# A planned attention and feed-forward kernel on one core: another build-time order for the first pairs, 26 early transfers begun by ScalarE, and one small VectorE instruction replaced

## The chip, the cores and the metric

The kernel runs on one NeuronCore of one Trainium2 chip. The metric is the device time of one execution in microseconds. Before the change it was 673.36, 673.85 and 676.03 us in three runs; the median is 673.85.

## What is computed

```python
batch, n_heads, seq, head_dim = (4, 8, 768, 48)
...
for t in range(S):
    kt, vt, bt = (k_n[:, :, t], v[:, :, t], beta[:, :, t, None])
    y[:, :, t] = np.einsum('bhd,bhde->bhe', q[:, :, t], state)
    v_old = np.einsum('bhde,bhd->bhe', state, kt)
    state = state + bt[:, :, :, None] * np.einsum('bhd,bhe->bhde', kt, vt - v_old)
...
h = x @ w_in
g = h * np.cos(h)
return (g @ w_out).astype(np.float32)
```

First comes a delta-rule attention: k_n is k divided by its norm plus 1e-6, and a state of 48 x 48 per batch and head is corrected at every one of the 768 steps. Its output, laid out as 3072 tokens of 384 numbers, is x of a feed-forward block with 2048 hidden columns and the gate h cos h. The feed-forward weights arrive as 64-bit floats, read as pairs of 32-bit words.

## The kernel before

**Units and pairs.** The sequence is cut into 24 units of 32 steps, and two units make a pair. Within a unit the recurrence is solved as a triangular system. For one pair the products of its keys (`gram`, L591) are scaled on VectorE (`gram_keys`, L602), written to DRAM (`gram_put`, L629) and fetched back in another layout (`gram_get`, L638); there a column-by-column elimination makes the inverse (`invert`, L667 and L674, 31 columns of two instructions each). It runs on VectorE for pair 0, and on GpSimd for all others. The result is written to DRAM (`put`, L683; for pair 0 ScalarE first copies it, L678) and fetched back for each unit (`get`, L692, four transfers). Then, on TensorE: `state` (old state times keys and queries, L709), `solve` (L740), `update` (L763), `within` (L780) and `features` (a transpose, L799). VectorE stands between them with the right side (L724), `u` (L750) and the new state (L771). So each unit waits for the one before it.

**Norms.** ScalarE squares k (L495), VectorE sums (L500), GpSimd takes the root (L512), and VectorE makes the scales; its first instruction there adds 1e-6 to the norm (L523, a tensor_scalar).

**Feed-forward.** A weight block comes in as word pairs (`narrow_load`, L460), is split on ScalarE (L468, L470), shifted on VectorE (L474, L479), and added on GpSimd (L483). There are 28 blocks: 0 to 11 are w_in, 12 to 27 are w_out. For pairs 0 and 1 the hidden layer is computed plainly (`hidden`, L820, eight blocks for each pair); block k of a unit needs the w_in adds up to 3k + 2. ScalarE and VectorE make the gate from it (`turns`, `rest`, `cos`, `gate`, L860 to L876). The output of pair 0 is plain too (`output`, L962): its first block of columns needs w_out adds 12 to 15. All later products use seven multiplications instead of eight, with sums made by VectorE (L936, L955, L1019, L1035).

**What sets the order.** Class `Order` is a planner that runs while the program is built. Every step is added with an engine, a cost, a due time and its dependencies. `run` plays the steps through, each time taking for a free engine the ready step that is due first, and emits the instructions in that order; at the end every instruction is tied to the one before it on its engine (`pin`). So each engine works through a fixed order, and the planner's costs and due times reach the chip only through it. `NUDGE` moves due times by kind of step, `STICK` lets TensorE stay with small-tile or with large steps a little longer, and transfers are modelled with eight in flight. All early transfers are issued by SyncE, except the first two q loads (eight transfers) on ScalarE and the constants on GpSimd. In the built program each transfer waits for the transfer that stands eight places before it, whichever queue began it. Tiles with tag `g` (eight buffers) are shared by the word pairs, the squares and the gates.

```python
    IN_FLIGHT, ISSUE = 8, 0.49
...
            for engine, heap in ready.items():
                if free[engine] > now:
                    continue
                able = [x for x in heap if x[0] <= limit and fits(x[2])]
                item = min(able, default=None)
```

Of the kernel before, what the change touches and what calls it, by code (L numbers as in the profile page):

```python
# [46 lines left out]
class Order:  # L47
# [9 lines left out]
    WINDOW = 818.445  # L57
    LAG = {"PE": 0.2, "DVE": 0.15, "ACT": 0.15, "POOL": 0.2, "SP": 2.0, "IN": 0.0}
    IN_FLIGHT, ISSUE = 8, 0.49
# [3 lines left out]
    STICK = 1.823  # L63
    CHANGE = 0.15

    EARLY, NUDGE = 6, {('state', True): -3.4, ('features', False): -48.4, ('left', True): 37.6, ('solve', True): -19.7, ('turn', False): 12.2, ('within', True): -6.1, ('features_out', True): 39.0, ('rest', False): -12.6, ('weigh', False): -49.2, ('gram_put', True): 12.6, ('collect', False): -26.2, ('within', False): -32.5, ('features', True): -14.4, ('gate', True): -24.7, ('layer_out', False): -12.4, ('update', True): -10.5, ('sum', False): 24.3, ('layer', False): -1.8, ('add', True): -24.4, ('cos', True): 15.7, ('update', False): -6.1, ('solve', False): -34.1, ('norms', True): -9.2, ('state', False): -9.6, ('sum', True): 20.5, ('right', True): 24.7, ('hidden', True): 17.1, ('blocks', False): 2.6, ('gram', False): -8.1, ('inv_out', False): -15.0, ('v', False): 17.4, ('out', True): -13.0, ('eye', True): -0.5, ('features_out', False): -17.0, ('within_out', False): -0.6, ('gram_get', False): 12.2, ('gram_get', True): -21.0, ('turns', True): 8.1, ('scale', True): 5.8, ('k', True): -20.2, ('shift', True): -4.8, ('shift', False): 2.4, ('collect', True): 0.5, ('out', False): 0.3, ('scale', False): -1.8, ('out_out', True): 0.9, ('weigh', True): 5.0, ('store', True): -5.1, ('split', False): 9.0, ('within_out', True): -1.7, ('turns', False): -10.9, ('store_right', True): 3.6, ('turn_out', True): 1.5, ('k', False): 0.9, ('store_right', False): -5.1, ('inv', False): 5.4, ('square', False): 7.4, ('square', True): 4.1, ('norms', False): -1.3, ('store', False): 3.3, ('hidden', False): -4.1, ('cos', False): 3.4, ('x_sum', False): -0.6, ('beta_home', False): -1.9, ('store_left', True): -3.3, ('get', False): -6.1, ('get', True): 4.0, ('in_sums', False): 2.9, ('gram_queries', True): 1.6, ('turn_out', False): 5.0, ('update_out', False): -0.3, ('store_left', False): 0.1, ('inv', True): 1.1, ('v', True): -0.9, ('eye', False): -2.2, ('x_sum', True): 0.7, ('split', True): -3.1, ('beta_home', True): -4.7, ('weights', True): -0.3, ('gate', False): -3.7, ('put', False): -1.3, ('inv_out', True): -1.1, ('gram_keys', True): 0.6, ('solve_out', False): -1.5, ('add', False): 1.0, ('in_sums', True): 0.3}
# [19 lines left out]
    def add(  # L86
        self, key, engine, cost, emit, deps=(), makes=(), uses=(), moves=0.0, due=1e9
    ):

        assert key not in self.tasks, key  # L90
        self.tasks[key] = [engine, cost, due, emit, set(deps), makes, uses, moves]
        for t in uses:
            self.users[t] = self.users.get(t, 0) + 1
        for tag, t in makes:
            self.tiles[t] = tag
# [7 lines left out]

    def stall(self, key, now, commit):
# [5 lines left out]
        for i in range(self.written + 1, self.written + n + 1):  # L110
            t = now + cost * (i - self.written) / n + stall
            if (i + self.PHASE + self.AHEAD) % self.BLOCK == 0:
                there[(i + self.PHASE + self.AHEAD) // self.BLOCK + 1] = t + self.FETCH
# [10 lines left out]
    def run(self, wrote):  # L124
# [16 lines left out]
        for key, task in self.tasks.items():  # L141
# [3 lines left out]
            task[2] += self.NUDGE.get((key[0], n < self.EARLY), 0.0)  # L145
# [6 lines left out]
        flights, dma_free, hot = [5.5] * 4 + [8.5] * 4, 8.0, 1e9  # L152
        running, small = {}, False
        events = [(t, 0, None, False) for t in sorted(set(free.values()) | {0.0})]
# [3 lines left out]
        while events:  # L158
# [28 lines left out]
            for engine, heap in ready.items():  # L187
                if free[engine] > now:
                    continue
                able = [x for x in heap if x[0] <= limit and fits(x[2])]  # L190
# [39 lines left out]
                if moves:  # L230
                    end, parts = now, max(1, round(cost / self.ISSUE))
                    for _ in range(parts):
                        end = max(end, flights[-self.IN_FLIGHT]) + self.ISSUE
                        dma_free = max(dma_free, end + 0.5) + moves / parts
                        flights.append(dma_free + 1.4)
                    done = flights[-1]
# [12 lines left out]
def kernel(  # L249
# [70 lines left out]
    def quarter(b):  # L320
        return slice(C * b, C * b + C)
# [31 lines left out]

    def load(n, what="kqv", eng=nc.sync):
# [52 lines left out]
    nc.vector.memset(halves, 0.5)  # L407
    halfpi = const.tile([128, 1], FP, name="halfpi")
# [47 lines left out]
    def narrow_load(t):  # L456
# [3 lines left out]
        nc.sync.dma_start(out=words[t], in_=src)  # L460
# [58 lines left out]
    def scale(m, part):  # L519
# [3 lines left out]
        nc.vector.tensor_scalar_add(knrm, knrm, 1e-6)  # L523
# [94 lines left out]
    def gram_put(n):  # L618
# [9 lines left out]
        for rows, heads, bs in parts:  # L628
            nc.sync.dma_start(  # L629
# [3 lines left out]
    def gram_get(m):  # L633
# [3 lines left out]
        for a in range(SPLIT):  # L637
            nc.sync.dma_start(  # L638
# [42 lines left out]
    def put(m):  # L681
        z_drs[m] = dram.tile([ROWS, SPLIT, 2, H, B, C], FP, name="z_dr")
        nc.sync.dma_start(  # L683
# [3 lines left out]
    def get(n):  # L687
# [3 lines left out]
        for b in range(B):  # L691
            nc.sync.dma_start(out=zts[n][quarter(b)], in_=z_dr[b])  # L692
# [403 lines left out]
    W_IN, W_OUT, LOADS = 24.824, 4.888, 290.255  # L1096
    ONES, PLAIN = range(2), range(1)
    outs_done, collected, layered = [None], [None], [None]
    START = 41.528
    FIRST, STEP = 2.12, 3.854  # L1100
    BASE = [START + (8 * FIRST + (p - 1) * 8 * STEP if p else 0) for p in range(NU // 2 + 2)]

    def inverse(m):
        add(("gram_get", m), "SP", 1.2, lambda: gram_get(m),
            [("gram_put", 2 * m), ("gram_put", 2 * m + 1)], makes=[("gb", ("gb", m))],
            uses=[("g_dr", m)], moves=1.6)
# [372 lines left out]
```

## Time and profile before

| what | value |
|---|---|
| median of three runs | 673.85 us |
| the profiled execution | 673.89 us |
| its span, first to last instruction | 672.1 us |
| TensorE busy | 612.8 us, 91% |
| VectorE, ScalarE, GpSimd busy | 476.5, 295.7, 346.5 us |
| granted TensorE clock, mean | 0.992 |
| moved by DMA | 52.56 MB in 215516 packets, 206948 of them under 512 B |
| instructions | 27308 |

The profiled execution took 1.8 us more than its span. A profile of this kind gives, for each engine, the time in which it executed something, so an engine that is not busy may be waiting or have nothing to do; the waits say for whom. "PEld" is the loading of weights into TensorE, which overlaps its products. A line number is that of the kernel printed above; with SyncE ("SPq") the lines are those of the issued transfers. The table of stretches gives busy microseconds of each engine between two points of the span. A wait named "issue" is one for which the profile shows no releaser.

### The profile page before, as it was taken

What the parts mean: (1) busy time and instruction counts of PE and PEld (TensorE: products, weight loads), DVE (VectorE), ACT (ScalarE), POOL (GpSimd) and SP (SyncE); (2) the same over time, 40 slices, a digit from 0 to 9 for tenths busy, and PEclk for the clock granted to TensorE, in tenths of its full rate; (3) what the DMA queues carried; (4) which work ended last, traced back from release to release, by engine and by line L of the source; (5) the groups of instructions that cost most, each with busy time, mean ns of one, the idle gap of its engine ahead of it and who ended that gap; (6) DMA issues with size and microseconds to landing.
All of it is one profiled execution on the core that took longest, in us unless ns stands there. A gap on an engine that the chain in (4) does not pass through costs nothing.

```text
span 672.1 us, 27308 instructions
## 1 busy us (share of the span) xinstructions
PE 612.8 (91%) x11864; PEld 573.4 (85%) x11864; DVE 476.5 (71%) x911; ACT 295.7 (44%) x510; POOL 346.5 (52%) x734
## 2 busy tenths in 40 slices
PE   4303798999999999999999999999999999999996
PEld 3203786896999998999999999999999999999996
DVE  5799588978676785886876876776666656656661
ACT  4432457672153543653443444444434434434530
POOL 4369878976858328586285482582481670000000
PEclk9999798999999999999999999999999999999999
DMA  8897755455463453534524524515213202000000
GB/s 180 200 207 163 171 116 154 115 98 92 70 101 63 68 87 63 101 44 69 106 39 64 110 33 66 109 25 90 52 22 60 52 6 55 1 5 24 1 24 24
DMA packets 215516, 52.56 MB, mean 78 GB/s; under 512 B 206948, under 2 KB 210164, under 8 KB 215396
## 3 DMA queue, kind: packets, MB, share of 16 engines
q1 hardware_dynamic: 212964, 49.98, 38.7%
q8 instruction: 93, 1.52, 0.9%
q10 hardware_dynamic: 2176, 0.39, 0.4%
q0 software_dynamic: 256, 0.44, 0.3%
q14 instruction: 27, 0.22, 0.1%
HBM read 39.76 MB, written 11.01 MB: 76 GB/s over the span
## 4 chain that ended last, share of the span: by engine, by line
PE 83%; SPq 4%; DMA 4%; POOL 3%; issue 2%; DVE 2%; ACT 1%; ACTq 0%; POOLq 0%
PE p_h L936 29%; PE p_out L1019 28%; PE p_h L820 5%; PE p_kq L709 4%; PE p_out L962 3%; PE p_s L763 3%; PE p_u L740 3%; PE p_kq L780 3%; PE p_g L591 2%; PE p_o L1019 2%; SPq L369 1%; PE p_z L799 1%; SPq L692 1%; POOL knrm L512 1%; DMA zt<-z_dr 1%
## 5 line engine op out<-in xcount | busy, mean ns | idle before, releaser
L667 POOL TENSOR_TENSOR part<-z,gb 128x126 f32<-128x126 f32 (+22 forms) x341 | 132.3, 388 | 108.2 <-DMA gb<-g_dr 47.0
L674 POOL TENSOR_TENSOR z<-z,part 128x126 f32<-128x126 f32 (+22 forms) x341 | 139.9, 410 | 26.7
L936 PE MATMUL p_h<-x_ffn,w_in 128*128 128x128 f32 x1120 | 143.6, 276 | 0.1
L936 PEld LDWEIGHTS p_h<-x_ffn,w_in 128*128 128x128 f32 x1120 | 135.5, 192 | 1.4 <-issue 0.2
L1019 PE MATMUL p_out<-w_out,g_ffn 128*128 128x192 f32 x672 | 123.8, 329 | 0.1
L1019 PEld LDWEIGHTS p_out<-w_out,g_ffn 128*128 128x128 f32 x672 | 107.5, 190 | 1.2
L860 ACT ACTIVATE turns<-p_h 128x512 int32<-128x512 f32 x96 | 56.9, 595 | 101.0 <-DVE p_h L955 74.6
L1019 PE MATMUL p_out<-w_sum,g_ffn 128*128 128x192 f32 x496 | 91.5, 329 | 0.0
L872 ACT ACTIVATE turns<-turns 128x512 f32<-128x512 f32 x96 | 60.4, 629 | 45.1 <-DVE turns L865 44.9
L1019 PEld LDWEIGHTS p_out<-w_sum,g_ffn 128*128 128x128 f32 x496 | 79.3, 190 | 0.9
L876 DVE TENSOR_TENSOR g_ffn<-turns,p_h 128x512 f32<-128x512 f32 x96 | 65.4, 682 | 18.8 <-ACT turns L873 18.0
L865 DVE SCALAR_TENSOR_TENSOR turns<-p_h,turns 128x512 f32<-128x512 f32 x96 | 65.5, 684 | 16.3 <-ACT turns L860 16.0
L1035 DVE TENSOR_TENSOR g_ffn<-g_ffn 128x512 f32<-128x512 f32 x88 | 62.6, 712 | 13.6 <-PE p_out L1019 13.0
L512 POOL TENSOR_TENSOR knrm<-ksum,halves 128x16 f32<-128x16 f32 (+1 forms) x14 | 36.3, 2598 | 66.8 <-DVE ksum L500 66.8
L873 ACT ACTIVATE turns<-turns,halfpi 128x512 f32<-128x512 f32 x96 | 69.3, 722 | 3.1
L955 DVE TENSOR_TENSOR p_h<-g_ffn,p_h 128x512 f32<-128x512 f32 x60 | 41.7, 695 | 38.8 <-PE p_h L936 32.8
L952 ACT COPY g_ffn<-p_h 128x512 f32<-128x512 f32 x60 | 35.0, 583 | 74.8 <-PE p_h L936 74.6
L820 PE MATMUL p_h<-x_ffn,w_in 128*128 128x128 f32 x384 | 48.3, 284 | 0.4 <-issue 0.4
L820 PEld LDWEIGHTS p_h<-x_ffn,w_in 128*128 128x128 f32 x384 | 45.7, 198 | 1.8 <-issue 0.8
L1069 DVE SCALAR_TENSOR_TENSOR o<-p_out,o 128x192 f32<-128x192 f32 x74 | 25.2, 353 | 26.3 <-PE p_out L1019 25.5
L936 PE MATMUL p_h<-x_sum,in_sum 128*128 128x128 f32 x320 | 43.7, 280 | 0.0
L936 PEld LDWEIGHTS p_h<-x_sum,in_sum 128*128 128x128 f32 x320 | 39.5, 191 | 1.1
(94 smaller groups left out, 784.9 us busy)
## 6 DMA issues: line engine op xcount, KB each, us to landing
pairs<-in_moe_w_in_dram SPq DMA_DIRECT2D x12, 512.0 KB
gb<-g_dr SPq DMA_DIRECT2D x24, 256.0 KB
pairs<-in_moe_w_out_dram SPq DMA_DIRECT2D x16, 384.0 KB
vp<-in_v_dram SPq DMA_DIRECT2D x96, 48.0 KB
out_dram<-o SPq DMA_DIRECT2D x23, 192.0 KB
z_dr<-z SPq DMA_DIRECT2D x12, 256.0 KB
zt<-z_dr SPq DMA_DIRECT2D x96, 32.0 KB
kp<-in_k_dram SPq DMA_DIRECT2D x128, 24.0 KB
```

Of the source, the lines that this page charges most:

```text
L512: nc.gpsimd.tensor_tensor(out=scales[m][2][:, part], in0=sums[m, part.start][:, 0:n], in1=halves[:, 0:n], op=ALU.pow,)
L667: eng.tensor_tensor(out=part, in0=z[:, 0:rows, j, None].to_broadcast(shape), in1=a[:, j, None, j + 1 :].to_broadcast(shape), op=ALU.mult,)
L674: eng.tensor_tensor(out=behind, in0=behind, in1=part, op=ALU.subtract)
L820: nc.tensor.matmul(p_h[:, i], w_in[:, t, (4 * k + i) * 128 : (4 * k + i + 1) * 128], xts[p][:, t, unit * 128 : (unit + 1) * 128], start=(t ...
L860: nc.scalar.activation(turns[p, f], hidden_of(p, f), AF.Copy, scale=TURN)
L865: nc.vector.scalar_tensor_tensor(out=r, in0=hidden_of(p, f), scalar=TURN, in1=t, op0=ALU.mult, op1=ALU.subtract,)
L872: nc.scalar.activation(r, r, AF.Abs)
L873: nc.scalar.activation(r, r, AF.Sin, bias=halfpi, scale=-2.0 * math.pi)
L876: nc.vector.tensor_tensor(out=place(p, f), in0=step_of(rests.pop((p, f)), f), in1=step_of(hidden_of(p, f), f), op=ALU.mult,)
L936: nc.tensor.matmul(p_h[:, e], in_sum[:, odd_tile, 4 * s + e] if a == "s" else w_in[:, a, f * 128 : (f + 1) * 128], x_sums[p][:, unit] if b ...
L1019: nc.tensor.matmul(p_o, left(p, part, a)[:, e % 4], right(e, b), start=(e == 0), stop=(e == FT // 2 - 1), skip_group_check=True,)
L1035: nc.vector.tensor_tensor(out=left(p, s, to), in0=left(p, s, one), in1=left(p, s, two), op=op)
```

## The change

The planner gets another model of the transfers (a ring of 128 descriptors for each queue in place of eight in flight), other costs for some steps, other due times (`START`, `FIRST`, `STEP`, `W_IN`, `W_OUT`, `LOADS`) and other nudges, now also for single steps. `HOLD` keeps 30 single steps back until a time of the planner's clock. `ON_ACT` names 14 early steps whose transfers ScalarE issues in place of SyncE: seven weight blocks (3, 6, 11, 14, 15, 17, 18), the products of units 1, 2 and 4, q of units 5 and 6, k of unit 6 and the fetch of the inverse for unit 3; these are 7 + 3 + 4 x 4 = 26 transfers. A transfer on ScalarE takes a place in ScalarE's fixed order, among its copies and activations. In `scale` the tensor_scalar that adds 1e-6 becomes a tensor_tensor with a small constant tile. What is computed stays the same, and so does the number of TensorE's instructions. The instruction order changes on every engine.

```diff
-    WINDOW = 818.445
+    WINDOW = 592.173
...
-    IN_FLIGHT, ISSUE = 8, 0.49
...
+    RING, ISSUE = 128, 0.49
+    DESCRIPTORS = {
+        "weights": 8, "gram_put": 64, "gram_get": 4, "put": 128, "blocks": 32, "store": 8,
+        "store_left": 8, "store_right": 8,
+    }
...
-    STICK = 1.823
+    STICK = 4.014
...
+    EARLY, NUDGE = 6, {('hidden', True): 23.4, ('state', 1): 53.7, ('out', False): 6.0, ('layer', False): 5.4, ('out', True): 36.1, ('features', True): -20.4, ('right', False): 20.3, ('right', True): -15.7, ('cos', 0, 0): 12.2, ('features', False): -5.2, ('rest', False): 23.3, ('left', False): 5.9, ('gram', False): 4.9, ('rest', True): 5.8, ('scale', False): 4.6, ('gate', True): 3.2, ('cos', True): 16.5, ('shift', True): -7.7, ('k', True): -11.2, ('gram_put', True): 18.9, ('x_sum', False): -4.5, ('update_out', False): -18.3, ('solve', False): -3.9, ('update_out', True): 9.5, ('gram_get', True): 17.1, ('square', False): -14.6}
...
+    ON_ACT = {('weights', 18): 1, ('gram_put', 4): 1, ('get', 3): 1, ('weights', 11): 1, ('weights', 3): 1, ('k', 6): 1, ('weights', 14): 1, ('q', 6): 1, ('q', 5): 1, ('weights', 15): 1, ('weights', 6): 1, ('gram_put', 1): 1, ('gram_put', 2): 1, ('weights', 17): 1}
+    HOLD = {('shift', 9): 59.85, ('put', 1): 88.63, ('gate', 0, 4): 91.71, ('norms', 3, 0): 92.59, ('shift', 3): 45.29, ('right', 1, 0): 91.24, ('q', 6): 41.87, ('norms', 4, 0): 91.21, ('add', 16): 91.93, ('v', 2): 50.43, ('add', 4): 64.6, ('k', 2): 9.18, ('square', 2, 0): 46.6, ('right', 2): 90.57, ('v', 1): 37.49, ('turn', 5): 81.55, ('k', 7): 57.3, ('eye', 0): 23.9, ('add', 9): 77.59, ('k', 5): 38.18, ('gate', 0, 2): 83.98, ('add', 1): 25.67, ('features_out', 1): 89.15, ('shift', 14): 80.74, ('in_sums', 3, 1): 93.95, ('solve', 1): 74.45, ('turn', 3): 20.17, ('beta',): 9.52, ('shift', 1): 17.33, ('gram_queries', 5): 95.02}
...
+        if key in self.ON_ACT:
+            assert moves
+            engine = "ACT"
...
+    def descriptors(self, key):
+        n = self.DESCRIPTORS.get(key[0], 16)
+        if key[0] in ("k", "gram_put") and key[1] >= 8:
+            n //= 2
+        return n
...
-                there[(i + self.PHASE + self.AHEAD) // self.BLOCK + 1] = t + self.FETCH
+                there[(i + self.PHASE + self.AHEAD) // self.BLOCK + 1] = (
+                    t + self.FETCH + (1.5 if t < self.STEADY else 0.0)
+                )
...
-            task[2] += self.NUDGE.get((key[0], n < self.EARLY), 0.0)
+            task[2] += self.NUDGE.get((key[0], n < self.EARLY), 0.0) + self.NUDGE.get(key, 0.0)
...
-        flights, dma_free, hot = [5.5] * 4 + [8.5] * 4, 8.0, 1e9
+        flights, accepted, hot = [(7.0, 8.0, 8, "SP")], {}, 1e9
...
-        events = [(t, 0, None, False) for t in sorted(set(free.values()) | {0.0})]
+        events = [(t, 0, None, False) for t in sorted({0.0, *free.values(), *self.HOLD.values()})]
...
-                able = [x for x in heap if x[0] <= limit and fits(x[2])]
+                able = [
+                    x for x in heap
+                    if x[0] <= limit and fits(x[2]) and self.HOLD.get(x[2], 0.0) <= now
+                ]
...
-                        end = max(end, flights[-self.IN_FLIGHT]) + self.ISSUE
-                        dma_free = max(dma_free, end + 0.5) + moves / parts
-                        flights.append(dma_free + 1.4)
-                    done = flights[-1]
+                        end = max(end, accepted.get(engine, 0.0))
+                        begin = max(flights[-1][1], end + 0.95)
+                        flights.append(
+                            (begin, begin + moves / parts, self.descriptors(key), engine)
+                        )
+                        accepted[engine], room = end + 0.3, self.RING
+                        for a, b, n, on in reversed(flights):
+                            if on != engine:
+                                continue
+                            if n > room:
+                                accepted[engine] = max(
+                                    accepted[engine], a + (b - a) * (n - room) / n
+                                )
+                                break
+                            room -= n
+                        end += self.ISSUE
+                    done = flights[-1][1] + 1.4
...
+    def queue(*key):
+        return nc.scalar if key in Order.ON_ACT else nc.sync
...
+    tiny = const.tile([128, 2, H], FP, name="tiny")
+    nc.vector.memset(tiny, 1e-6)
...
-        nc.sync.dma_start(out=words[t], in_=src)
+        queue("weights", t).dma_start(out=words[t], in_=src)
...
-        nc.vector.tensor_scalar_add(knrm, knrm, 1e-6)
+        nc.vector.tensor_tensor(out=knrm, in0=knrm, in1=tiny[:, 0:n], op=ALU.add)
...
-            nc.sync.dma_start(
+            queue("gram_put", n).dma_start(
...
-            nc.sync.dma_start(
+            queue("gram_get", m).dma_start(
...
-        nc.sync.dma_start(
+        queue("put", m).dma_start(
...
-            nc.sync.dma_start(out=zts[n][quarter(b)], in_=z_dr[b])
+            queue("get", n).dma_start(out=zts[n][quarter(b)], in_=z_dr[b])
...
-    W_IN, W_OUT, LOADS = 24.824, 4.888, 290.255
+    W_IN, W_OUT, LOADS = -26.491, -112.0, 248.614
...
-    START = 41.528
-    FIRST, STEP = 2.12, 3.854
+    START = -14.528
+    FIRST, STEP = 4.445, 3.402
...
-        add(("gram_get", m), "SP", 1.2, lambda: gram_get(m),
+        add(("gram_get", m), "SP", 1.0, lambda: gram_get(m),
...
-            uses=[("g_dr", m)], moves=1.6)
+            uses=[("g_dr", m)], moves=1.8)
...
-                lambda x=x: load(n, x), deps,
+                lambda x=x: load(n, x, queue(x, n)), deps,
...
-            add(("scale", m, a), "DVE", 1.2, lambda: scale(m, part),
+            add(("scale", m, a), "DVE", 1.1, lambda: scale(m, part),
...
-            add(("weigh", m), "DVE", 1.0 if n < PLAIN_TURNS else 1.35, lambda: weigh(m),
+            add(("weigh", m), "DVE", 1.1 if n < PLAIN_TURNS else 1.5, lambda: weigh(m),
...
-            add(("turn", n), "PE", 0.9, lambda: turn(n, tag),
+            add(("turn", n), "PE", 1.0, lambda: turn(n, tag),
...
-        few = 0.75 if n < PLAIN_TURNS else 0.52
+        few = 0.75 if n < PLAIN_TURNS else 0.66
...
-        add(("features", n), "PE", 0.35, lambda: features(n), [("within_out", n)],
+        add(("features", n), "PE", 0.4, lambda: features(n), [("within_out", n)],
...
-        c = 1.0 if t < 12 else 0.8
+        c = 1.0 if t < 12 else 0.78
...
-            makes=[("g", ("pairs", t))], moves=1.65 * c, due=LOADS + 2 * t)
+            makes=[("g", ("pairs", t))], moves=1.8 * c, due=LOADS + 2 * t)
...
-    add(("beta_home",), "DVE", 0.5, spread_beta_home, [("beta",), ("gram_get", 0)])
+    add(("beta_home",), "DVE", 0.8, spread_beta_home, [("beta",), ("gram_get", 0)])
...
```

More of the change, by code (lines that the diff above doesn't have):

```diff
@@ L47 @@
 class Order:
-    WINDOW = 818.445
+    WINDOW = 592.173
     LAG = {"PE": 0.2, "DVE": 0.15, "ACT": 0.15, "POOL": 0.2, "SP": 2.0, "IN": 0.0}
-    IN_FLIGHT, ISSUE = 8, 0.49
+    RING, ISSUE = 128, 0.49
[3 more added lines that the diff above has]
+    }
     STEADY, LATE = 130.0, {"SP": 3.0, "POOL": 2.0}
     SLOW, WARM = 1.7, 4.0
-    STICK = 1.823
+    STICK = 4.014
     CHANGE = 0.15
-    EARLY, NUDGE = 6, {('state', True): -3.4, ('features', False): -48.4, ('left', True): 37.6, ('solve', True): -19.7, ('turn', False): 12.2, ('within', True): -6.1, ('features_out', True): 39.0, ('rest', False): -12.6, ('weigh', False): -49.2, ('gram_put', True): 12.6, ('collect', False): -26.2, ('within', False): -32.5, ('features', True): -14.4, ('gate', True): -24.7, ('layer_out', False): -12.4, ('update', True): -10.5, ('sum', False): 24.3, ('layer', False): -1.8, ('add', True): -24.4, ('cos', True): 15.7, ('update', False): -6.1, ('solve', False): -34.1, ('norms', True): -9.2, ('state', False): -9.6, ('sum', True): 20.5, ('right', True): 24.7, ('hidden', True): 17.1, ('blocks', False): 2.6, ('gram', False): -8.1, ('inv_out', False): -15.0, ('v', False): 17.4, ('out', True): -13.0, ('eye', True): -0.5, ('features_out', False): -17.0, ('within_out', False): -0.6, ('gram_get', False): 12.2, ('gram_get', True): -21.0, ('turns', True): 8.1, ('scale', True): 5.8, ('k', True): -20.2, ('shift', True): -4.8, ('shift', False): 2.4, ('collect', True): 0.5, ('out', False): 0.3, ('scale', False): -1.8, ('out_out', True): 0.9, ('weigh', True): 5.0, ('store', True): -5.1, ('split', False): 9.0, ('within_out', True): -1.7, ('turns', False): -10.9, ('store_right', True): 3.6, ('turn_out', True): 1.5, ('k', False): 0.9, ('store_right', False): -5.1, ('inv', False): 5.4, ('square', False): 7.4, ('square', True): 4.1, ('norms', False): -1.3, ('store', False): 3.3, ('hidden', False): -4.1, ('cos', False): 3.4, ('x_sum', False): -0.6, ('beta_home', False): -1.9, ('store_left', True): -3.3, ('get', False): -6.1, ('get', True): 4.0, ('in_sums', False): 2.9, ('gram_queries', True): 1.6, ('turn_out', False): 5.0, ('update_out', False): -0.3, ('store_left', False): 0.1, ('inv', True): 1.1, ('v', True): -0.9, ('eye', False): -2.2, ('x_sum', True): 0.7, ('split', True): -3.1, ('beta_home', True): -4.7, ('weights', True): -0.3, ('gate', False): -3.7, ('put', False): -1.3, ('inv_out', True): -1.1, ('gram_keys', True): 0.6, ('solve_out', False): -1.5, ('add', False): 1.0, ('in_sums', True): 0.3}
```

## The prediction

> **What bounds the kernel now.** I read first the busy times and the forty slices, to see which engine is full and where it is not.
>
> ```profile
> PE 612.8 (91%) x11864; PEld 573.4 (85%) x11864; DVE 476.5 (71%) x911; ACT 295.7 (44%) x510; POOL 346.5 (52%) x734
> ...
> PE   4303798999999999999999999999999999999996
> ...
> DMA  8897755455463453534524524515213202000000
> ```
>
> TensorE is idle for 672.1 - 612.8 = 59.3 us, and the digits put nearly all of that into the first seven slices. The same split, by stretches that I chose at the first solve (59.6), the end of the first output block (95.4) and the point where TensorE is full:
>
> ```profile
> 0.00:59.60 59.60, 14.26 (x297) 11.48 (x298) 46.29 (x127) 21.82 (x39) 33.81 (x52) 1.00 0.88 191
> 59.60:95.40 35.80, 31.06 (x822) 27.23 (x822) 26.23 (x46) 18.30 (x34) 32.24 (x44) 0.90 0.63 143
> 95.40:118.00 22.60, 19.59 (x449) 16.36 (x450) 18.26 (x39) 14.66 (x29) 16.12 (x30) 0.92 0.61 158
> 118.00:134.00 16.00, 16.00 (x272) 14.14 (x274) 14.77 (x25) 9.41 (x19) 14.51 (x26) 1.00 0.42 107
> 134.00:640.00 506.00, 504.78 (x9862) 477.36 (x9862) 357.68 (x655) 225.45 (x383) 249.79 (x586) 1.00 0.34 59
> ```
>
> (Columns: stretch, length, then busy PE, PEld, DVE, ACT, POOL; last the granted clock, the DMA engines' share, GB/s.) TensorE idles 45.3 us before the first solve, 4.7 to 95.4, 3.0 to 118, then only 1.2 in 506 us. From 134 on TensorE alone sets the time, so the change counts only by how much TensorE work is done by then. Up to 59.6 the DMA engines are 88% busy; from 59.6 to 95.4 GpSimd is 90% busy. TensorE's waits name the places:
>
> ```profile
> PE p_u L740 <- DMA zt<-z_dr: 25.6, 3, 25.0
> ...
> PE p_kq L709 <- issue: 2.5, 1, 2.5
> PE p_t L560 <- issue: 1.5, 1, 1.5
> PE p_s L763 <- DVE u L750: 1.3, 1, 1.3
> ```
>
> (Total, times, longest.) The long one is the first inverse coming back from DRAM. SyncE's timeline shows its way:
>
> ```profile
> 48.03 0.39 SPq L683 DMA_DIRECT2D z_dr<-z  x1
> 48.51 4.25 SPq L369 DMA_DIRECT2D qp<-in_q_dram  x4
> 52.80 1.94 SPq L369 DMA_DIRECT2D vp<-in_v_dram  x4
> 54.83 0.39 SPq L460 DMA_DIRECT2D pairs<-in_moe_w_in_dram  x1
> 55.27 4.23 SPq L692 DMA_DIRECT2D zt<-z_dr  x8
> ```
>
> VectorE inverts from 27.91 to 46.02, ScalarE copies until 46.70, the put goes out at 48.03, the get at 55.27, and the solve starts at 59.59: 13.6 us after the inverse. Four q loads took 4.25 us there against 1.95 for four others, so SyncE was held.
>
> **What the Trainium skill says.** (1) "DMA: Bandwidth & Descriptors", section "Issuing engines are not separate DMA queues": transfers begun by ScalarE run on the same 16 engines, and a second issuer saves only sequencer time. The 88% agrees that issue is not the main limit. (2) Same page, "Queues, rings and completion order": SP and ACT own one row each, served in turn; so a ScalarE transfer need not wait behind SyncE's backlog. The trace of before, with eight early ScalarE transfers, cannot show it. (3) "SBUF — State Buffer", "Who interferes with whom": tensor_scalar in a two-port mode contends with GpSimd, and tensor_tensor with two SBUF inputs contends with GpSimd's reads too. The trace agrees on both: L523 took 1.25 us instead of 0.17 behind a GpSimd add, and L531, a TENSOR_TENSOR, once took 0.90 instead of 0.19.
>
> **The change, part by part.** The planner runs at build time and costs the chip nothing; only the order and the queues count. Stretches: front (to the first solve), middle (to the first output block), rest.
>
> *Front, SyncE.* In the built order 73 SyncE transfers stood before the first put; now 57: twelve (products of units 1 and 2, weights 3 and 6, q of unit 5, k of unit 6) go to ScalarE, and four v loads fall behind the put. At 0.49 us each that is 16 x 0.49 = 7.8 us of issue, but the bytes still pass 88% busy engines, and in the built program every transfer waits for the one eight before it, on either queue. So only what was held counts. Put at 46.7 instead of 48.03: 1.3. The q loads unheld: 4.25 - 1.95 = 2.3. The first get no longer shares an eight-transfer burst with the second, perhaps 1.5. Bounds 0 and 5.1; I take 2.3. Product 1 goes out on the emptier row and weights 3 no longer stands ahead of the fetch: the inverse can start at most 27.91 - 26.70 = 1.2 earlier, as VectorE works till 26.70; I take 0.7. Sum 3.0, from -2 (ScalarE late with the copy, rival 3) to 6.3: first solve at 56.6.
>
> *Front, ScalarE.* It gains 26 transfers, 26 x 0.49 = 12.7 us. ScalarE is busy 54.8 of the first 118 us, so there is cover. Just ahead of the inverse's copy (L678 before) stand eight of them, q of unit 6 and k of unit 6. Behind them queue that copy, the put and the solve. They can begin when weights 6 is split, about 39, and paired with SyncE's eight v and k loads need some 4 to 5 us: done by 44, the inverse ends at 45.3. Cost 0, cover about 1.
>
> *knrm add, L523 to tensor_tensor with `tiny`.* Fourteen instructions; two were held 1.08 us each. By (3) the new form can be held too. Bounds 0 and 2.2 (the inverse's start above already caps it); I take 0. The added memset is 0.07 us, before VectorE's first wait of 5 us: nothing.
>
> *Middle, GpSimd.* The order now puts nine w_in adds and two w_out adds inside the second inverse (L667/L674), and two more w_out adds directly after it. Before, four w_in adds and one root lay inside it: 77.83 - 37.74 = 40.1 us, of which adds 6.5 and root 2.9, so the inverse alone is 30.7. Now TensorE's first output block needs w_out adds 12 to 15, which are done only then: 30.7 + 9 x 1.52 + 4 x 1.10 + 2.9 = 51.7 us after its start. Its start is the landing of the second fetch. On SyncE 15 transfers now lie between the two fetches, were 12: +1.5 us, less some 0.5 for the earlier first fetch: 38.7. So the first output can start at 38.7 + 51.7 = 90.4.
>
> TensorE's own line to that point, with the trace's durations: solve 2.0, wait for u 1.25, update 1.6, within 1.5, y copied 0.7, features 0.8, issue hold 2.5, state 1.9, gram 1.2, hidden 5.0 (clock still low) and 2.8, solve 0.9, hidden 2.9, update and within 1.7, turn 1.2, state 1.4, features 0.5, hidden 2.9: 32.8, thus 56.6 + 32.8 = 89.4. The page "TensorE: Matmul & The Clock Gate", Part 1, says that the clock is low until TensorE has been busy for a while; the 0.83 of the stretch 59.6 to 79.5 agrees, and I leave that cost as it was. GpSimd is later by 1.0, so **GpSimd, not the first solve, sets the middle**. Output 90.4 to 93.2, plus the gram of unit 5 (0.86), which before had done by then: 94.0 against 95.4. **Gain 1.4** (bounds -1.5 and 4.4: GpSimd's pieces swing by 3).
>
> *Rest to 134.* Before lost 3.0 more. The new order has seven hidden blocks ahead of the third solve where four stood, so TensorE has work while inverses return. VectorE takes over as the tight one: it reaches gram 5 early, waits, and then has about 12.5 us ahead of u of unit 2, some 0.6 after TensorE wants it. Gain 3.0 - 0.6 = 2.4.
>
> *Whole run.* TensorE's instructions are the same in number. Small-tile groups and large ones change place 166 times, were 172; a block after small tiles takes 2.88 instead of 2.68 us, so 3 returns x 0.2 = 0.6. The last nine output blocks stand alike: the tail is unchanged. In the steady stretch gets stand as close to their solves as before, where the waits were 0.2 and 0.4: 0.
>
> Sum: 1.4 + 2.4 + 0.6 = 4.4 to 4.6 us. The profiled execution took 673.9 (span 672.1 and 1.8 around it), which is the median of the runs, 673.85. **Predicted 669.3.**
>
> **Rivals.** (1) *Middle line moves on*: GpSimd and VectorE, at 90% and more, take everything that the order gives; the idle of 7.7 after 59.6 reappears as waits for adds and u. For it: VectorE 14.8 of 16 us at 118. Against: VectorE idles 9.6 of 35.8 to 95.4. Only the 0.6 and about 1 remain: 672.3. (2) *Front opens*: second fetch at 36, adds uncontended (1.28 as at 22.28, not 1.52; 9 x 0.24 = 2.2): output at 86 to 87, some 4 us more gain: 665. (3) *Slower*: ScalarE is in order, and its eight loads ahead of the inverse's copy wait for transfers of SyncE. If they are held beyond the inverse's end, put, get and solve move with them; and the four w_out loads behind that, placed among turns and cos, wait for buffers that GpSimd frees. Price: one hold as seen on SyncE is 2.3; two on the chain to the solve and two among the turns, 9.2, less the 4.5: 678.6. It decides once ScalarE's cover of about 1 us at 44 is gone. For it: the rule of eight ties the two queues. Against: ScalarE is 37% busy till then. (4) *The order changes, the bottleneck does not*: the same bytes in another order at 88%: 673.9.
>
> **How the numbers follow.** Forecast 0.50 (own range 667 to 671.5); rival 1 0.19; rival 2 0.15; rival 3 0.10; rival 4 0.06. About 0.5% (3.4 us, so 670.5 and 677.2) is what a measurement of this kernel can tell from no change. Faster: 0.85 of the forecast and rival 2, 0.58. Same: the rest of the forecast, rivals 1 and 4, a little of 3: 0.34. Slower 0.08. Low 664 takes in most of rival 2, high 675 rivals 1 and 4, leaving out about 0.15.
>
> **What would show it.** Right: first solve at 55 to 58; first output block near 90, released by a GpSimd w_out add; GpSimd's second inverse starting at 38 to 39; TensorE idle under 5 us from 59 to 134; the stretch after 134 full. Wrong: the inverse's copy on ScalarE later than 0.3 us after the inverse; turns waiting behind ScalarE's transfers; a first solve at 59 or later; TensorE waits after 134 of over 2 us.

## The result and the profile after

The changed kernel is **slower**: 683.57 us (median of 4 runs, 681.75 to 684.08), against 674.82 us for the kernel before in the same session (4 runs, 673.36 to 676.03). The ratio is 1.0132, with a 95% interval of 1.0105 to 1.0158. The prediction was 669.3. The profiled execution took 681.75 us, its span is 680.0.

The page of the changed kernel, the lines that answer to those shown of before:

```profile
PE 612.3 (90%) x11864; PEld 572.5 (84%) x11864; DVE 474.5 (70%) x912; ACT 293.8 (43%) x510; POOL 348.3 (51%) x734
...
PE   4302889989999999989999999999999999999997
...
DMA  8887655753354462453434533525303302000000
```

TensorE is as busy as before, and idle for 680.0 - 612.3 = 67.7 us where it was 59.3: the loss of 7.9 us of span is waiting. The stretches of the prediction, the last one cut at 300 (columns as there):

```profile
0.00:59.60 59.60, 14.48 (x296) 11.48 (x296) 42.06 (x126) 22.38 (x40) 28.96 (x44) 1.00 0.84 188
59.60:95.40 35.80, 28.83 (x755) 25.50 (x756) 26.78 (x43) 15.29 (x29) 33.13 (x50) 1.00 0.57 141
95.40:118.00 22.60, 20.72 (x425) 17.45 (x426) 21.20 (x44) 17.47 (x34) 17.92 (x24) 1.00 0.60 146
118.00:134.00 16.00, 16.00 (x400) 15.42 (x388) 13.03 (x22) 10.88 (x21) 14.33 (x25) 1.00 0.72 139
134.00:300.00 166.00, 158.10 (x3180) 142.47 (x3178) 120.90 (x223) 69.88 (x121) 102.78 (x226) 1.00 0.47 80
300.00:640.00 340.00, 339.25 (x6601) 325.61 (x6602) 232.97 (x425) 148.91 (x255) 151.21 (x369) 1.00 0.28 49
```

and of the kernel before, from 134 to 300:

```profile
134.00:300.00 166.00, 165.41 (x3365) 151.95 (x3370) 124.19 (x231) 75.28 (x129) 106.52 (x238) 1.00 0.47 80
```

By 134 us TensorE has done 14.48 + 28.83 + 20.72 + 16.00 = 80.0 us of work, before 80.9: the forecast of 3.8 us more did not come. From 134 to 300 it idles 166.00 - 158.10 = 7.9 us, before 0.6. **Most of the loss lies in the stretch that the prediction had put at nothing.** TensorE's waits from 134 us on (total, times, longest):

```profile
PE p_u L781 <- DMA zt<-z_dr: 2.9, 2, 2.7
PE p_kq L750 <- issue: 1.9, 5, 0.8
PE p_h L861 <- DVE g_ffn L917: 1.2, 1, 1.2
PE p_g L632 <- ACT x_ffn L848: 0.8, 1, 0.8
PE p_h L977 <- DVE g_ffn L917: 0.4, 2, 0.2
PE p_h L977 <- issue: 0.4, 1, 0.4
PE p_u L781 <- issue: 0.3, 1, 0.3
PE p_g L632 <- issue: 0.3, 1, 0.3
PE p_kq L821 <- issue: 0.2, 1, 0.2
```

Three kinds stand out. Each has a place in a timeline.

**The get of pair 5 (2.7 us).** GpSimd ended that inverse at 278.0. SyncE's timeline:

```profile
278.00 5.48 SPq L408 DMA_DIRECT2D kp<-in_k_dram  x8
283.53 1.91 SPq L408 DMA_DIRECT2D vp<-in_v_dram  x4
285.54 1.71 SPq L670 DMA_DIRECT2D g_dr<-g  x3
287.36 0.54 SPq L724 DMA_DIRECT2D z_dr<-z  x1
...
294.87 5.56 SPq L733 DMA_DIRECT2D zt<-z_dr  x8
```

The put (L724) went out 9.3 us after the inverse, behind eight k loads, four v loads and three writes; the get followed at 294.87, and TensorE's solve, due at 297.6, began at 300.3. Before, the inverse of pair 5 ended at 278.9, and the put left 1.3 us later:

```profile
277.24 2.84 SPq L629 DMA_DIRECT2D g_dr<-g  x3
280.19 0.54 SPq L683 DMA_DIRECT2D z_dr<-z  x1
...
283.62 4.91 SPq L692 DMA_DIRECT2D zt<-z_dr  x8
```

**Waits named issue (2.8 us to 300, in eight pieces).** One of them in TensorE's timeline:

```profile
232.35 1.21 PE L750 MATMUL p_kq<-st,kq_t 48*32 48x48 f32 x108
234.32 0.36 PE L750 MATMUL p_kq<-st,kq_t 48*32 48x48 f32 x20 [0.76 <-issue]
```

It falls inside one group of products, all of one kind, with no releaser in the trace. I counted TensorE's instructions in the built program: all eight gaps lie at number 195 or 196 modulo 256. The DMA view from 231 to 234 us has the fetch:

```profile
q8 instruction: 1, 0.02, 2.3%
```

One packet of 16 KB of the instruction queue, from 231.79 to 232.90; TensorE went on 1.4 us after its end, and so after each of the other seven fetches (1.2 to 1.5 us). Over the whole span the page has 93 such packets, 1.52 MB, for 11864 products and as many weight loads. The Trainium skill, page "Advanced Engine Details and Errata", section "ISA Cache", says that a cache line of 16 KB holds 256 instructions; the trace agrees. The page "Runtime: NRT & Kernel Launch", section "Instruction fetch mechanics", calls the cost of crossing such a boundary mostly hidden; here it isn't where small products go by as fast as in the first line above, 108 products and as many weight loads in 1.21 us.

**Two waits at 136.8 and 144.0 (0.8 and 1.2 us)**, for a copy of x and for a gate. Both stand on ScalarE behind the splits of the last two weight blocks, for which ScalarE waited 1.9 and 3.4 us:

```profile
136.14 0.56 ACT L509 ACTIVATE w_out<-pairs 128x384 f32<-128x384 f32 x1 [1.91 <-DMA pairs<-in_moe_w_out_dram]
...
141.37 0.56 ACT L509 ACTIVATE w_out<-pairs 128x384 f32<-128x384 f32 x1 [3.37 <-DMA pairs<-in_moe_w_out_dram]
```

### The profile page after: what moved, and what is told of

Read it like the earlier page. It is cut to its first block, busy times and chain, and to the rows that moved or that the text cites. A ratio compares the mean times of both kernels' runs of the same rounds, so it can differ in the third digit from the quotient of the medians.

```text
span 680.0 us, 27316 instructions
## 1 busy us (share of the span) xinstructions
PE 612.3 (90%) x11864; PEld 572.5 (84%) x11864; DVE 474.5 (70%) x912; ACT 293.8 (43%) x510; POOL 348.3 (51%) x734
## 3 DMA queue, kind: packets, MB, share of 16 engines
q8 instruction: 93, 1.52, 1.0%
## 4 chain that ended last, share of the span: by engine, by line
PE 78%; DMA 8%; SPq 6%; DVE 3%; issue 2%; ACT 1%; POOL 1%; ACTq 0%; DVEq 0%
PE p_h L977 27%; PE p_out L1060 27%; PE p_kq L750 4%; PE p_h L861 4%; SPq L408 3%; PE p_s L804 3%; DMA qp<-in_q_dram 3%; PE p_kq L821 3%; PE p_u L781 3%; DMA pairs<-in_moe_w_in_dram 2%; PE p_g L632 2%; PE p_out L1003 2%; PE p_o L1060 2%; SPq L419 1%; PE p_z L840 1%
## 5 line engine op out<-in xcount | busy, mean ns | idle before, releaser
L708 POOL TENSOR_TENSOR part<-z,gb 128x126 f32<-128x126 f32 (+22 forms) x341 | 138.2, 405 | 127.5 <-DMA gb<-g_dr 63.1
L715 POOL TENSOR_TENSOR z<-z,part 128x126 f32<-128x126 f32 (+22 forms) x341 | 137.7, 404 | 26.7
L901 ACT ACTIVATE turns<-p_h 128x512 int32<-128x512 f32 x96 | 57.3, 596 | 75.1 <-DVE p_h L996 54.5
L906 DVE SCALAR_TENSOR_TENSOR turns<-p_h,turns 128x512 f32<-128x512 f32 x96 | 65.6, 685 | 17.9 <-ACT turns L901 17.6
L996 DVE TENSOR_TENSOR p_h<-g_ffn,p_h 128x512 f32<-128x512 f32 x60 | 41.7, 695 | 31.6 <-PE p_h L977 30.2
L977 PE MATMUL p_h<-x_sum,in_sum 128*128 128x128 f32 x320 | 42.3, 278 | 0.0
```

What stands on the lines that cost most here:

```text
L708: eng.tensor_tensor(out=part, in0=z[:, 0:rows, j, None].to_broadcast(shape), in1=a[:, j, None, j + 1 :].to_broadcast(shape), op=ALU.mult,)
L715: eng.tensor_tensor(out=behind, in0=behind, in1=part, op=ALU.subtract)
L901: nc.scalar.activation(turns[p, f], hidden_of(p, f), AF.Copy, scale=TURN)
L906: nc.vector.scalar_tensor_tensor(out=r, in0=hidden_of(p, f), scalar=TURN, in1=t, op0=ALU.mult, op1=ALU.subtract,)
L977: nc.tensor.matmul(p_h[:, e], in_sum[:, odd_tile, 4 * s + e] if a == "s" else w_in[:, a, f * 128 : (f + 1) * 128], x_sums[p][:, unit] if b ...
L996: nc.vector.tensor_tensor(out=block(p, s, 0, 1) if i == 3 else p_h, in0=block(p, s, *one), in1=p_h, op=ALU.add,)
```

## The experiments

My **theory S** was: the late order (after 134 us) costs most, by these three kinds of wait. **Rival E**: the early order makes later pairs late, and the waits after 134 are its echo. **Rival A**: the transfers on ScalarE are to blame. Most runs keep the planner's steps and replay a list of them, so that single steps can be moved and nothing else is planned anew:

```diff
-    log = order.run(wrote)
+    for n in SEQUENCE:
+        task = order.tasks[named[n]]
+        task[3]()
+        wrote([tag for tag, _ in task[5]])
```

In e1, e2, e6 and e9 the planner's own order stays. All runs in one table: the ratio to the kernel before on the same chip with its 95% interval, and TensorE's busy time in two stretches of the one profiled execution. The expectations in microseconds were set against 674.82; in the runs below the kernel before took 671.3 to 672.9, so go by the ratios. One execution can lie well off the median of its kernel: that of e3 took 671.62 us, its median is 675.45.

| run | ratio | 95% | to 134 | 134 to 300 |
|---|---|---|---|---|
| before | 1 | | 80.9 | 165.4 |
| changed | 1.0132 | 1.0105-1.0158 | 80.0 | 158.1 |
| e1 changed, all on SyncE | 1.0121 | 1.0091-1.0152 | 79.5 | 161.1 |
| e2 before, 26 on ScalarE | 1.0042 | 1.0023-1.0061 | 80.2 | 164.6 |
| e3 early changed, late before | 1.0063 | 1.0041-1.0084 | 82.3 | 164.1 |
| e4 early before, late changed | 1.0105 | 1.0073-1.0137 | 82.1 | 160.9 |
| e5 changed, put and gets of pair 5 moved | 1.0108 | 1.0072-1.0144 | 81.2 | 160.0 |
| e6 before, block boundaries shifted | 1.0102 | 1.0054-1.0151 | 83.5 | 164.4 |
| e7 as e3, all on SyncE | 1.0068 | 1.0048-1.0088 | 80.3 | 162.7 |
| e8 changed, TensorE steps spread | 1.0177 | 1.0141-1.0213 | 82.0 | 159.0 |
| e9 before with tensor_tensor | 1.0009 | 0.9984-1.0033 | 82.4 | 164.2 |
| e10 changed, second fetch moved | 1.0128 | 1.0096-1.0159 | 81.2 | 158.8 |
| e11 changed, last weights moved | 1.0117 | 1.0091-1.0143 | 81.0 | 159.6 |
| e12 as e3, with the moves of e10, e11 | 1.0071 | 1.0043-1.0098 | 80.0 | 163.1 |
| e13 changed, three mends | 1.0119 | 1.0089-1.0149 | 80.3 | 159.7 |
| e14 front changed, rest before | 1.0062 | 1.0040-1.0085 | 78.5 | 165.4 |
| e15 middle changed, rest before | 1.0040 | 1.0024-1.0057 | 82.2 | 163.2 |

**e1 and e2, ScalarE's transfers alone.** The first lines are the edit of e1; the kernel before gets `ON_ACT` and `queue` in e2, used in the same five places as in the change.

```diff
-        return nc.scalar if key in Order.ON_ACT else nc.sync
+        return nc.sync
...
+    def queue(*key):
+        return nc.scalar if key in Order.ON_ACT else nc.sync
...
-        nc.sync.dma_start(out=words[t], in_=src)
+        queue("weights", t).dma_start(out=words[t], in_=src)
```

> The changed kernel in its own order, but the 26 early transfers go out on SyncE again, each at the same place of the emitted order. Theory S (the loss sits in the order of the steps after 134 us: stalls of TensorE at its own instruction fetches, and a put and get queued behind loads): 681 to 685 us, as the changed kernel, and the idle of TensorE from 134 to 300 stays near 7.9 us. Rival A (ScalarE's transfers hold its copies and turns, and the rest follows): 674 to 677 us. Rival E (the later second inverse moves every later pair, an echo of the early order): 681 to 685 us too.

> The kernel before in its own order, but the same 26 early transfers are begun by ScalarE, each at the same place of the emitted order. Theory S and rival E: within 2 us of the kernel before, 673 to 677 us. Rival A: 679 us or more, with the inverse's copy or the turns on ScalarE waiting behind transfers.

Measured: 1.0121, so without ScalarE's transfers the changed order is as slow as with them; rival A falls as the main cause. One part of S's forecast missed: TensorE idles 4.9 us from 134 to 300, not 7.9, since the wait for pair 5 is only 0.5 us in that execution, with no step moved. So that wait isn't a fixed price of the order. In the order of before ScalarE's transfers cost 0.42%, more than S allowed. A part of it shows in TensorE's timeline of e2:

```profile
57.80 1.92 PE L744 MATMUL p_u<-vp,zt 32*32 32x48 f32 x64 [22.72 <-DMA zt<-z_dr]
63.69 1.56 PE L767 MATMUL p_s<-u,kp 64*64 64x96 f32 x32 [3.97 <-DVE u L754]
```

and of before:

```profile
59.59 2.01 PE L740 MATMUL p_u<-vp,zt 32*32 32x48 f32 x64 [25.04 <-DMA zt<-z_dr]
62.86 1.56 PE L763 MATMUL p_s<-u,kp 64*64 64x96 f32 x32 [1.25 <-DVE u L750]
```

ScalarE's transfers did bring the first solve 1.8 us forward. But the update that follows came 0.8 us *later*: VectorE, in order, had shifts of weights and other steps ahead of u and reached it at 62.53 (before at 61.70). **What ends last there is VectorE's queue, not the first solve.** The 0.8 us are less than a third of the 0.42%; where the rest goes isn't traced.

**e3 and e4, early and late order apart.** The steps up to 130 us of the plan (135 to 136 us on the chip) in one kernel's order, all others in the other's; as lists, for e3 and then for e4:

```diff
-SEQUENCE = changed
+SEQUENCE = changed[plan < 130] + [step in before, if not yet done]
...
-SEQUENCE = before
+SEQUENCE = before[plan < 130] + [step in changed, if not yet done]
```

> The steps of the changed kernel in its order up to 130 us of the plan (about 136 us on the chip), with its transfers on ScalarE; all remaining steps in the order of the kernel before. Theory S: the late loss goes, 674 to 677 us (before plus the 0.9 us that the early part lost). Rival E: the late pairs stay late, 681 to 685 us. Rival A: 680 us or more as well.

> The kernel before up to 130 us of its plan, all on SyncE; all remaining steps in the order of the changed kernel. Theory S: the late loss comes with the late order alone, 679 to 683 us. Rival E and rival A: nothing late is lost, 673 to 676 us.

The late order alone costs 1.05%, and TensorE's 2.7 us wait for pair 5 is there with its early part untouched: it is no echo, so rival E falls for the late part. But the early order alone costs 0.63% too, more than the 0.9 us that one profile had shown. S was half the story. The two add to 0.0168, a little over the 0.0132 of both together, which their intervals allow.

**e6, the block boundaries.** Nothing is reordered; 36 tiny products of a small tile that VectorE zeroes first stand ahead of TensorE's first real step.

```diff
+    bank_0 = bank("h", [128, 512], "bank_0")
+    for _ in range(36):
+        nc.tensor.matmul(bank_0[0:16, 0:16], zero, zero)
```

> The kernel before, every step in its own order; ahead of TensorE's first product, while it is idle anyway, stand 36 tiny products of a zeroed tile that nobody reads (144 instructions). They move the places at which TensorE's instruction stream crosses into the next block of 256 by 144 instructions. Theory S (TensorE's short waits named issue are instruction fetches that come late where small products run fast): the waits of that name after 134 us rise from 0.24 us to between 5 and 9 us, ratio 1.007 to 1.013. Rival (they have another cause, tied to the steps themselves): within 0.2 us of 0.24, ratio 1.000.

TensorE's waits after 134 us in e6, and then in the kernel before:

```profile
PE p_g L597 <- issue: 4.9, 4, 2.1
PE p_u L746 <- issue: 1.6, 2, 1.1
```

```profile
PE p_u L740 <- DMA zt<-z_dr: 0.6, 2, 0.4
PE p_u L740 <- issue: 0.2, 1, 0.2
```

They rose from 0.2 to 6.5 us with no step, wait or queue changed, all at number 195 or 196 modulo 256 of the new count, and the time by 1.02%. In this profile the solve of unit 10 still came earlier than before, at 294.87 against 295.94, so the added products at the start are not what cost the time. These waits are TensorE's own instruction fetch, and the order of before had been fitted to where the boundaries fall. The planner has a term for them: its method `stall` reckons with blocks of 256 instructions and a fetch of 3.5 us, and passes over a step that would stall by more than 0.3 us while another is ready. The 144 instructions take the order off the places that it had reckoned with. That the changed order meets such stalls without any shift shows that this reckoning does not always hold on the chip.

**e5, e8, e11, e13, mending the late waits.** The edits as orders of steps: SyncE's in e5 and e11, one of the twelve places of TensorE's order in e8. e13 makes the moves of e5 and e11, and has four of the tiny products of e6.

```diff
-k 17, v 13, gram_put 13, put 5, blocks 16 (k), blocks 16 (q), gram_get 6, store, get 10, get 11
+put 5, k 17, get 10, get 11, v 13, gram_put 13, blocks 16 (k), gram_get 6, blocks 16 (q), store
...
-blocks 8 (k), blocks 8 (q), weights 26, k 11, weights 27
+blocks 8 (k), weights 26, blocks 8 (q), weights 27, k 11
...
-gram 11, out, state 8, out
+gram 11, out, out, state 8
```

> The changed kernel; only five SyncE steps are moved: the put of pair 5 ahead of the k loads of unit 17 (its inverse ends at 278.0 and the put went out at 287.4), the two gets of that pair right behind these loads, and the fetch of pair 6 one step up. Theory S: the 2.7 us that TensorE waited for the get at 297.6 are gone and nothing takes their place at once: 0.3 to 0.4% less than the changed kernel, a ratio to the kernel before of about 1.009. Rival M (TensorE's order is bound by something else right behind it, and the wait only moves on): 1.012 to 1.014.

> The changed kernel; only TensorE's order is touched: twelve times, between 188 us and the end, one small-tile step and the large step beside it change places, so that a long run of small products no longer ends at a block boundary of the instruction stream (25 places of TensorE's order differ, no other engine's order). Theory S: of the 3.2 us of issue waits after 134 us some 1.7 go (those at 189.4, 233.6, 276.9 and 507.9), ratio to before 1.009 to 1.011. Rival: they stay or are replaced by waits of the same sum, ratio 1.012 to 1.014.

> The changed kernel; only the last two weight loads are moved on SyncE: block 26 ahead of the second half of the block loads of unit 8, block 27 ahead of the eight k loads of unit 11. Theory W (ScalarE stands at the splits of these blocks, 1.9 and 3.4 us, while turns and a copy of x wait behind them, and TensorE waits 0.8 and 1.2 us for those at 137 and 145): both waits of TensorE go, up to 2 us, ratio 1.010 to 1.013. Rival: VectorE is late there by itself, and a wait of over 0.7 us stays near 145.

> The changed kernel with three mends at once: the put and gets of pair 5 earlier, the last two weight loads earlier, and four tiny products of a zeroed tile ahead of TensorE's first, which move its block boundaries by 16 instructions (in a count of how fast TensorE runs through the 294 instructions ahead of each boundary, that offset leaves the changed order about 2 us less of late fetches). Theory S: the mends add up, 1.9 + 1.7 + 2 = 5.6 us, ratio 1.0132 - 0.0083 = 1.005, between 1.003 and 1.008. Rival M (behind each wait stands the next one, so that mends don't add up): 1.009 to 1.013.

Each single move takes away the wait that it aims at. In e11 the wait at 137 is gone and 0.3 us is left of that at 144, and TensorE does 65.0 instead of 63.4 us of work from 134 to 200. In e5 and e13 no solve waits for pair 5. In e8 the four boundaries that it aimed at stall no more. But the time hardly follows. The times of e5 and e11 decide nothing by themselves: both ratios lie within the interval of the changed kernel, but that of e5 (1.0072 to 1.0144) also holds the 1.009 of theory S, and 1.0117 is what theory W allowed for e11. **All mends together give 1.0119, rival M.** One of the three did nothing there: with the boundaries moved by 16 instructions the waits named issue after 134 us still sum to 3.1 us, as in the changed kernel. So e13 tests two mends, for which S forecast 1.9 + 1.7 = 3.6 us, a ratio of about 1.008; its interval, 1.0089 to 1.0149, leaves that out by little. TensorE's timeline of e13 where the get was late:

```profile
288.17 1.16 PE L983 MATMUL p_h<-x_ffn,in_sum 128*128 128x128 f32 x8 [1.80 <-ACT g_ffn L999]
...
295.91 1.41 PE L1066 MATMUL p_out<-w_sum,g_ffn 128*128 128x192 f32 x7 [1.30 <-DVE o L1116]
```

and ScalarE's:

```profile
280.31 0.60 ACT L907 ACTIVATE turns<-p_h 128x512 int32<-128x512 f32 x1
285.53 0.84 ACT L542 ACTIVATE ksq<-kp 128x768 f32<-128x768 f32 x1 [4.62 <-DMA zt<-z_dr]
```

TensorE is 2.1 us further on here than in the changed kernel (it begins the same group of output products at 283.6, there at 285.7), but the k loads are not: they are issued from 276.49 to 283.66, there from 278.00 to 283.48, and ScalarE's square of that k starts at 285.53, there at 285.56 (I take it to wait for k; the releaser named above, a get, is only the last transfer before it). The copy L999, for which TensorE waits, stands behind the square. The v loads come 4.1 us later, and VectorE's o waits behind the scaling of v. SyncE issues with hardly a pause from 276 to 298, so what goes second there makes somebody wait. **In all eight profiles with the changed late order the solves of units 8 and 10 lie 42.2 to 43.8 us apart, though TensorE works only 39.8 to 40.4 us between them:** 2.0 to 3.7 us of waiting stay, under changing names. e8 is a miss: the swapped steps came before their operands (three waits for x_ffn, 1.9 us to 300), other boundaries stalled (1.1 us at 262.7, 0.9 at 455.1), and it is the slowest of all.

**e7, e10, e12, e14, e15, what the early order costs.** The edit of e10 in SyncE's order, then the lists of e14 and e15; e7, e14 and e15 have all transfers on SyncE, as e1.

```diff
-v 0, weights 5, q 4, gram_get 1
+v 0, weights 5, gram_get 1, q 4
...
+SEQUENCE = changed[plan < 60] + [step in before, if not yet done]
...
+SEQUENCE = before[plan < 60] + [step in changed[plan < 130], if not yet done] + [step in before, if not yet done]
```

> As the run with the changed early order and the late order of before (ratio 1.0063), but with the 26 transfers back on SyncE. If ScalarE's transfers are what the early part costs (in the order of before they cost 0.4%): ratio 1.000 to 1.003. If the early order itself costs it (the second inverse some 4 us late, the put of pair 1 at 92 instead of 78): 1.005 to 1.008.

> The changed kernel; only the second fetch (pair 1) is moved, ahead of the four q loads of unit 4. There it no longer stands eight places behind a weight load of 512 KB that landed at 37.2 us. Theory F (that place holds the fetch; the second inverse then sets the middle): fetch issued near 32 instead of 37.2, second inverse near 38 instead of 43.1, put of pair 1 near 89 instead of 94, and TensorE gets 2 to 4 us more work done by 134 us: ratio 1.007 to 1.010. Rival V (TensorE's and VectorE's own lines bind the middle, the inverse had room): the inverse is earlier, TensorE's work by 134 us is not, ratio 1.011 to 1.014.

> The changed early order with both moves (the second fetch ahead of the q loads, the last two weight loads earlier), and from 130 us of the plan on the order of the kernel before. If the early part's cost of 0.6% is made of these two waits: ratio 0.997 to 1.001, and the changed early order is then as good as that of before or better. If not: 1.003 to 1.007.

> The changed order up to 60 us of the plan (about the first solve), the order of before from there on, all transfers on SyncE. If the front carries the early loss: ratio 1.005 to 1.008, as with the changed order up to 130. If the middle carries it: 0.997 to 1.002, since the first solve comes about 1 us earlier.

> The order of before up to 60 us of the plan, the changed order from 60 to 130, the order of before again from there on, all transfers on SyncE. If the middle carries the early loss (more steps of VectorE and ScalarE ahead of the gates, so that TensorE waits for a gate near 145): ratio 1.005 to 1.008. If the front carries it: 0.998 to 1.003.

e7 equals e3 within their intervals: it isn't ScalarE's transfers. e10 tests the second fetch. SyncE issued it at 37.21 in the changed kernel, in the moment in which a weight load of 512 KB, issued at 31.63 and eight transfers ahead of it, had landed. Moved ahead of the q loads it went out at 31.6, and GpSimd's second inverse began at 39.0 instead of 43.1:

```profile
39.04 0.24 POOL L708 TENSOR_TENSOR part<-z,gb 128x31 f32<-128x31 f32 x1 [12.75 <-DMA gb<-g_dr]
```

Its put left at 90.3 instead of 94.1. TensorE gained nothing: 81.2 us of work by 134, within the 80.0 to 82.3 of the other profiles of this early order with ScalarE's transfers, and 1.0128. Rival V: the inverse had room. e12, 1.0071, agrees: these two waits are not what the early part costs. Front (e14) and middle (e15) cost 0.62% and 0.40% alone and 0.68% together (e7); together they cost less than their sum, but the difference is no larger than the noise of three ratios. The 1.0040 of e15 lies between its two forecasts. In e14 TensorE waits 3.1 us for the state from VectorE and 2.0 us for y from ScalarE between the first and the second solve; in e3, e7, e12 and e15 it waits 1.0 to 1.9 us for a gate between 142.7 and 146.5.

**e9, the small VectorE instruction.**

```diff
-        nc.vector.tensor_scalar_add(knrm, knrm, 1e-6)
+        nc.vector.tensor_tensor(out=knrm, in0=knrm, in1=tiny[:, 0:n], op=ALU.add)
```

> The kernel before, with only the addition of 1e-6 done by the tensor_tensor with a small constant tile. Every theory: no difference that can be measured, ratio 0.998 to 1.002; single instructions of the new form can still be held by GpSimd, since the changed kernel's trace has one of 1.25 us among others of 0.15.

1.0009: no difference that can be measured, as the prediction had it. The new form is held just as the old one was: in this profile two additions took 1.25 us each, at 17.9 and 22.6, and in the kernel before two took 1.25 and 1.24, at 17.7 and 22.3; most others took about 0.17.

## Why the prediction was wrong, step by step

**"In the steady stretch gets stand as close to their solves as before ... 0": wrong, by 7.3 us in the profile.** This is the largest failed step. I compared distances in TensorE's order, not when SyncE would get to the put: 9.3 us behind the inverse of pair 5 where it was 1.3. And I took the stretch's full TensorE as given, though its order decides where runs of small products meet the block boundaries; no step of mine asked what the waits named issue were, though two of them stood in the lines that I showed and the planner's `stall` reckons with them. e4 shows that the late order alone costs 1.05%; e6 that boundaries alone can cost 1.0%.

**Front, "put at 46.7", "q loads unheld 2.3", "first solve at 56.6": half right, and beside the point.** In the profile the put left at 48.17 and the solve came at 60.42; in the eight profiles with this early order and ScalarE's transfers, the solve came between 57.3 and 60.8, mean 58.9, against 59.4 to 60.7 with the early order of before. The q loads were held longer, 5.66 us. The sign that I had set for rival 3 showed: the inverse ended at 46.67, and ScalarE's copy waited for its k transfers:

```profile
44.84 2.62 ACTq L408 DMA_DIRECT2D kp<-in_k_dram  x4
47.56 0.59 ACT L719 COPY z<-p_i 128x512 f32<-128x512 f32 x1 [6.00 <-DMA kp<-in_k_dram]
```

So the cover of about 1 us was gone. But e1 shows that this isn't what made the kernel slow.

**"wait for u 1.25": 2.55.** This term of TensorE's line used up what the first solve had gained. VectorE's timeline of the changed kernel:

```profile
61.56 1.25 DVE L564 TENSOR_TENSOR knrm<-knrm,tiny 128x16 f32<-128x16 f32 x1 [1.18 <-POOL knrm L553]
...
63.85 1.02 DVE L791 TENSOR_TENSOR u<-p_u,bz 128x384 f32<-128x384 f32 x2
```

The new order puts the scales of the next pair, which wait for GpSimd's root, ahead of the first u; their first instruction is the new tensor_tensor, held for 1.25 us. I carried the wait of before over to an order in which something else stands in front. In the eight profiles named under the front the first update began at 62.4 to 65.2, against 62.4 to 63.9 with the early order of before and its transfers on SyncE: the earlier solves brought no earlier update.

**"GpSimd, not the first solve, sets the middle": wrong.** The second inverse began at 43.10, not 38.7, since I had counted fifteen transfers by issue time and not seen which one stands eight places ahead. The output began at 93.47 (forecast 90.4) without waiting for an add; only its second half did, for 0.2 us:

```profile
95.12 1.89 PE L1003 MATMUL p_out<-w_out,g_ffn 128*128 128x384 f32 x4 [0.20 <-POOL w_out L524]
```

e10 brought the inverse 4.1 us forward and gained nothing. "Gain 1.4" and "2.4" became a loss of 0.9 in the profile, and of 0.4 to 0.7% in the timed runs e3, e7, e14 and e15.

**L523, cost 0:** right (e9). **Switches, 0.6:** TensorE's busy time fell from 612.8 to 612.3, but profiles of these kernels differ by more than that, so it isn't shown. **Tail unchanged:** right: from 640 to its end TensorE idles 5.0 us in both kernels. **The sum:** its three terms give 4.4, and the 669.3 was taken from 4.6; that is 0.2 us of an error of over 14.

**The rivals.** Rival 1 (the middle line moves on) describes the early part, but it had the late part unhurt. Rival 3 had the sign (678.6) by another mechanism than the one that acted.

**What stays open.** The late cost of 1.05% comes with the late order (e4), but the mends move its waits on, and no run shows what paces them. That the changed order solves unit 8 at 257.0 instead of 244.2 and unit 10 at 300.3 instead of 295.9, so that one round of loads has 43 us instead of 52, is an explanation from the traces that no run isolates. In the early part it isn't settled which step of VectorE or ScalarE costs the 0.4 to 0.7%.

## What to carry to other kernels

When a new order is judged from a trace of the old one, a duration may be carried over, a wait may not: ask for each in-order queue what now stands ahead of the step, SyncE's transfers in the stretch that is "full" included. An engine that looks full can be full because its order was fitted to something that the profile leaves unnamed; find out what every wait named issue is before you call a stretch safe. And when a wait is mended, look at what is second on the same queue before you count the gain.

## What the runs showed of the hardware

TensorE can stall on its own instruction stream. Every 256 instructions a packet of 16 KB is fetched; after 134 us in the changed kernel it took 0.9 to 1.5 us. In each of the eight stalls to 300 us TensorE went on 1.2 to 1.5 us after the packet's end. These boundaries came 3.4 to 5.1 us after the one before, but such a distance alone does not make a stall: the boundary at 168.2 came 4.0 us after its predecessor and was passed without one, its packet having ended 2.1 us earlier. The stalls were 0.2 to 0.8 us long (in e6 up to 2.1). The profile calls such a wait issue and names no releaser.

The tensor_scalar and the tensor_tensor that add 1e-6 were both held up to 1.25 us, where most took about 0.17 (kernel before and e9).
